# Runs of four: channels and key features interleaved by fours, and sums moved from VectorE to TensorE

## The chip, the core and the metric

One core of a Trainium2 chip runs the whole program. The metric is the device time of one execution in microseconds (us), smaller is better. The engines named are TensorE (PE in the profile; PEld is its weight load), VectorE (DVE), ScalarE (ACT), GpSimd (POOL) and SyncE (SP), which issues the DMAs.

## What is computed

Two branches on the same input `x` (2048 positions, 512 channels, bf16), mixed by a gate per position:

```python
g = sigmoid((x * gate_w).sum(-1))
# A: a convolution along the sequence with a kernel K generated from 128 complex modes per channel
K[d, l] = Re( sum_n C[d,n] * exp(dt[d] * A[d,n] * l) * dt[d] * B[d,n] )
a = causal_conv(x, K) + x * Dskip                 # by FFT of length 4096
# B: linear attention, 32 heads of 16 channels
q, k, v = split(x @ wqkv);  pq, pk = q @ w_phi, k @ w_phi
phi(p) = concat(softmax(p), softmax(-p))          # 16 + 16 features of a head
kv = phi(pk)^T v;  z = phi(pk).sum(over positions)
b = (phi(pq) @ kv) / (phi(pq) @ z + 1e-6) @ wo
out = g * a + (1 - g) * b
```

## The kernel before, in words

The program is written as a plan of 1058 small nodes, each with an engine, its dependences and the buffers that it takes. A string written out by hand, `ORDER` (lines 74 to 95), gives the order in which all nodes are emitted, and so the order of the instructions on each engine; further strings say for some nodes which of two engines (`SIDES`) or which ring of PSUM banks (`RINGS`) they use. Each engine runs its own list strictly in order: an instruction that waits holds up all that stand behind it on that engine.

In order of time, the work is:

- *Preparation* (0 to 30 us): trigonometric tables, transposed input `xT`, folded weights `WW` (`w_phi` multiplied into the key part of `wqkv`).
- *Keys* (`attention_keys`, line 660; 30 to 75 us for the most part, the last pieces at 103 us). Eight passes `s2`, each over two tiles (`u`) of 128 positions. For a tile, `pk` (line 709) is four products of 512 columns into a PSUM bank of the ring `bk` (three banks); `ek` (715) is two exps on ScalarE, of +p and of -p, into the tile's `Ek`. The softmax needs the sum of each head's 16 features. The node `zp` with `ps4` (723) and the node `zk` with `rd` (732) form it, in one of two ways, chosen for each pass by a digit of `ZPS` = "01000111". Digit 1: TensorE adds up four of the sixteen by products with the identity (8 products of 256 columns, line 730), and VectorE reduces the 512 values that are left (739). Digit 0: `zp` issues nothing, and VectorE reduces the 1024 values of each of the two tiles (736). Then `rz` (744): Ln and Exp on ScalarE, the reciprocal of the sums. `vp` (757) is the value product, `vb` its copy, `vr` (766) the values times the reciprocals, and `kn` (774) the 32 products of a tile that add phi(k)^T v into `kvp`, 32 columns of `Ek` as weights each.
- In between, the *input's transform*: `udc` (576) copies half of the channels of the input, with the channels split in two halves `e`, into `UDp`; `psAu` (591) multiplies it with the first FFT stage, 128 columns of `UDp` as weights; `XAu`, `psBu` and `xst` follow, and the result goes to DRAM.
- *Polar tables* (75 to 103 us): `Ctab` and `Dtab`, factors of the convolution kernel's modes, by ScalarE and VectorE. They begin with a ScalarE table load (`tabT`), which in the order stands behind the last `rz` of the keys but one part.
- *Kernel generation and convolution* (103 us to the end). Sixteen units of 32 channels. For a unit, VectorE makes the left factor `A` as two products of 2048 elements, `a1` (1100) and `a2` (1105), and the right factor `R` as two more (1117, 1121) from `E` and `cs`. The product over the modes has four terms. Where the unit's digit in `FOURS` is 1 (units 1, 2, 3, 4, 7, 9, 11 and 12), TensorE adds all four, 128 small products `kps` (line 183, 32 columns of `A` as weights, 64 columns of `R`). Where it is 0 (units 0, 5, 6, 8, 10, 13, 14 and 15), `a3` (1110) first adds the two halves of `A` on VectorE, and TensorE needs 64 products. `KD`, `psA`, `XA`, `psB`, `XK` and `t` (1231) apply the FFT stages and multiply with the input's transform; `psz`, `Zr`, a trip through DRAM (`Zd`, `ZT`) and `psy` turn it back. The attention's query side (`pq`, `Eq`, `zs`, `apm`, `ax`, `ops`) runs between the units, and the output is written at the end.

In memory, `A` is [2 x 2 terms, 4, 8, 32 channels]: the 32 weights of one channel are 32 bf16 values (64 bytes) apart. `UDp` is [2, 64, 32 channels], so its 128 weights are 64 bytes apart too. `Ek` is [2 tiles, 2 signs, 512]: its weights are adjacent.

Of the kernel before, what the change touches and what calls it, by code (L numbers as in the profile page):

```python
# [10 lines left out]
ACT = mybir.ActivationFunctionType  # L11
ALU = mybir.AluOpType
F32 = mybir.dt.float32
BF16 = mybir.dt.bfloat16
# [56 lines left out]
class Plan:  # L71
# [27 lines left out]
             "01111")  # L99
    WARM = ("000000000000000000000000000000000000000000000000000000000000000000000000000000000000000000000000000000000000000000000000"  # L100
            "000000000000000000000")
    FOURS = ("0111100101011000")
    ZPS = ("01000111")

    HOT = ("pk", "vp", "pq", "zp", "ops", "bps4", "psA", "psBu", "psB128", "psB64", "psB32", "psz", "pszn", "psyn32", "psy128", "psy64", "psy32", "kps")

# [68 lines left out]
def kgen_chunk(nc, kps, A, R, four):  # L175

    for e in range(2):
        for g4 in range(4):
            terms = [(k, k) for k in range(2)] if not four else [(0, 0), (2, 0), (1, 1), (3, 1)]
            for i, (ka, kr) in enumerate(terms):  # L180
                for dj in range(4):
                    d = 8 * g4 + 4 * e + dj
                    nc.tensor.matmul(kps[32 * dj:32 * dj + 32, g4, e, :], lhsT=A[:, ka, :, :, d].rearrange("p a b -> p (a b)"),  # L183
                                     rhs=R[:, kr, d, :], start=(i == 0), stop=(i == len(terms) - 1), tile_position=(0, 32 * dj), skip_group_check=True)


# [373 lines left out]
def keys_and_spectrum(P, nc, g, psum):  # L560

    fc, act, at, xT = g.fc, g.act, g.at, g.xT
# [9 lines left out]
    for h in range(2):  # L572
        X = Bag()
        en, uc = [], []
        for k in range(4):
            def cu(h=h, k=k, X=X):
                if k == 0:
                    X.u = g.xau.tile([128, 2, 64, 32], BF16, name="UDp", tag="UDp", bufs=1)
                o = X.u[:, :, 16 * k:16 * k + 16, :].rearrange("p e t c -> p t e c")
                P.copy(o, g.UD[:, 16 * k:16 * k + 16, 64 * h:64 * h + 64].rearrange("p t (e c) -> p t e c", e=2))  # L580
            uc.append(P.add(("DVE", "ACT"), "udc", cu, [sx] + uc[-1:], take=(["UDp"] if k == 0 else []), rw=(f"ud{k}", "")))
        for g4 in range(8):
            box = Bag()

            def pa(h=h, g4=g4, box=box, X=X):
                if g4 == 0:
                    X.t = g.xau.tile([128, 2, 32, 4, 32], BF16, name="XAu", tag="XAu")
                box.ps = psum([128, 4, 256], "psA")
                for i in range(4):
                    c = 4 * g4 + i  # L590
                    nc.tensor.matmul(box.ps[:, i, :], lhsT=X.u[:, :, :, c].rearrange("p e t -> p (e t)"), rhs=fc.W1[:].rearrange("p i r d -> p (i r d)"),  # L591
                                     start=True, stop=True)

            def ea(g4=g4, box=box, X=X):
                i = box.ps[:].rearrange("p c x -> p x c")
                box.ps = None
                return X.t[:, :, :, :, 4 * g4:4 * g4 + 4].rearrange("p i r d c -> p (i r d) c"), i
                if g4 == 7:
                    X.u = None
            a = P.add("PE", "psAu", pa, [a] if g4 else uc, take=["ps"] + (["XAu"] if g4 == 0 else []), drop=(["UDp"] if g4 == 7 else []), rw=("W1", ""))  # L600
            en.append(evict("XAu", ea, [a]))
        eo = []
        for r0 in range(0, 32, 4):
            box = Bag()
# [21 lines left out]
            def wr(h=h, r0=r0, box=box):  # L626
                for n, a in ((128, 0), (64, 128)):
                    nc.sync.dma_start(out=g.XUd[:, h, a:a + n, r0 - 4:r0 + 4, :].rearrange("d x r c -> x d (r c)"), in_=box.s[0:n].rearrange("p d r c -> p d (r c)"))
                box.s = None
            a = P.add("PE", "psBu", pb, en + [a], take=["ps"] + (["xst"] if r0 % 8 == 0 else []), rw=(f"TB0{r0 // 16} TB1{r0 // 16} TBn", ""),  # L630
                      drop=(["XAu"] if r0 == 28 else []))
# [28 lines left out]
def attention_keys(P, nc, g, psum, r):  # L660

    fc, act, at, xT = g.fc, g.act, g.at, g.xT
# [17 lines left out]
    a = P.add("PE", "gps", ga, xt, take=["ps"], rw=("wsm", ""))  # L680
    b = P.add("DVE", "g_b", gb, [a], drop=["psum"])
    b = P.add("ACT", "g_e", lambda: act(out=G.z[:], in_=G.z[:], func=ACT.Exp, scale=-1.0), [b], tab="L")
# [13 lines left out]
    a2 = P.add("PE", "zps", gd, [b] + xt, take=["ps"], rw=("atm", ""))  # L696
# [4 lines left out]
    for s2 in range(8):  # L701
        K = Bag()
        red = []
        for u in range(2):
            box = Bag()
            def pk(st=2 * s2 + u, box=box):
                box.ps = bank("pk")
                for kt in range(4):
                    nc.tensor.matmul(box.ps[:], lhsT=xT[:, st, kt, :], rhs=g.WW[:, kt, :], start=(kt == 0), stop=(kt == 3))  # L709

            def ex(u=u, K=K, box=box):
                if u == 0:
                    K.E = g.kwk.tile([128, 2, 2, 512], BF16, name="Ek")
                for sg in range(2):
                    act(out=K.E[:, u, sg, :], in_=box.ps[:], func=ACT.Exp, scale=(1.0 if sg == 0 else -1.0))
                box.ps = None

            a = P.add("PE", "pk", pk, [a] if u else [sp] + xt + kp, take=["bk"] + ([] if u else ["Ek", "Zk", "vr"]), rw=("TBn", ""))
            x = P.add("ACT", "ek", ex, [a] + ([x] if u else []), drop=["psum"], tab="L")
            red.append(x)  # L720
        box = Bag()

        def ps4(K=K, box=box, on=P.ZPS[s2] == "1"):
            if not on:
                return
            box.ps = bank("zk")
            for u in range(2):
                e = K.E[:, u].rearrange("p g (h a b) -> p (g h) a b", a=4, b=4)
                for k in range(4):
                    nc.tensor.matmul(box.ps[:, 256 * u:256 * u + 256], lhsT=g.ident[:], rhs=e[:, :, k, :], start=(k == 0), stop=(k == 3), skip_group_check=True)  # L730

        def rd(K=K, box=box, on=P.ZPS[s2] == "1"):
            K.Z = g.kwk.tile([128, 2, 2, 32], F32, name="Zk")
            if not on:
                for u in range(2):
                    nc.vector.tensor_reduce(out=K.Z[:, u].rearrange("p g h -> p (g h)"), in_=K.E[:, u].rearrange("p g (h f) -> p (g h) f", f=16),
                                            axis=mybir.AxisListType.X, op=ALU.add)
                return
            nc.vector.tensor_reduce(out=K.Z[:].rearrange("p u g h -> p (u g h)"), in_=box.ps[:].rearrange("p (z b) -> p z b", b=4), axis=mybir.AxisListType.X, op=ALU.add)
            box.ps = None  # L740
        z = P.add("PE", "zp", ps4, red + [a], take=["bk"])
        red = [P.add("DVE", "zk", rd, [z], drop=["psum"])]
# [6 lines left out]
        l = P.add("ACT", "rz", rc, red, drop=["Zk"], tab="L")  # L749
        for u in range(2):  # L750
            box = Bag()
# [18 lines left out]
            def kn(u=u, st=st, K=K):  # L770
                for i in range(8):
                    sg, m = i // 4, i % 4
                    for pr in range(4):
                        nc.tensor.matmul(g.kvp[32 * pr:32 * pr + 32, i, :], lhsT=K.E[:, u, sg, 128 * m + 32 * pr:128 * m + 32 * pr + 32],
                                         rhs=K.v[:, u, sg, :, 8 * m + 2 * pr:8 * m + 2 * pr + 2], start=(st == 0 and i == 0), stop=(st == 15),
                                         tile_position=(0, 32 * pr), skip_group_check=True)
                if u == 1:
                    K.E = K.v = None
            a = P.add("PE", "vp", pv, [a], take=["bk", "vb"], rw=("wv", ""))
            c = evict("vb", cv, [a])  # L780
            c = P.add("DVE", "vr", sc, [c, l], drop=["vb"])
# [278 lines left out]
def plan_conv(P, nc, g, psum, r):  # L1060
# [6 lines left out]
    T, on, yn, late = {}, [], [], []  # L1067
# [20 lines left out]
    def kgen(units, XA, new, split=False):  # L1088
        K = Bag()
        K.done, kps, nu = [], [], len(units)  # L1090
        for cc, U in enumerate(units):
# [3 lines left out]
            c = Bag()  # L1095
            d0 = 32 * U

            def a1(c=c, d0=d0, U=U):
                c.A = g.wk.tile([128, 4, 4, 8, 32], BF16, name="A", tag="A", bufs=g.P.k["A"])
                nc.vector.tensor_tensor(out=c.A[:, 0:2].rearrange("p o a b c -> p (o a) b c"),  # L1100
                                        in0=g.C[U // 8][:, 0:2, :, d0 % 256:d0 % 256 + 32].rearrange("p o a c -> p (o a) c").unsqueeze(2).to_broadcast([128, 8, 8, 32]),
                                        in1=g.D[:, 0, :, d0:d0 + 32].unsqueeze(1).to_broadcast([128, 8, 8, 32]), op=ALU.mult)

            def a2(c=c, d0=d0, U=U):
                nc.vector.tensor_tensor(out=c.A[:, 2:4].rearrange("p o a b c -> p (o a) b c"),  # L1105
                                        in0=g.C[U // 8][:, 1:3, :, d0 % 256:d0 % 256 + 32].rearrange("p o a c -> p (o a) c").unsqueeze(2).to_broadcast([128, 8, 8, 32]),
                                        in1=g.D[:, 1, :, d0:d0 + 32].unsqueeze(1).to_broadcast([128, 8, 8, 32]), op=ALU.mult)

            def a3(c=c):
                nc.vector.tensor_tensor(out=c.A[:, 0:2], in0=c.A[:, 0:2], in1=c.A[:, 2:4], op=ALU.add)  # L1110
            an = [P.add("DVE", "A1", a1, [sh], take=["A"], rw=(Ck + " " + Dk, ""))]
            an.append(P.add("DVE", "A2", a2, an[-1:]))
            an.append(P.add("DVE", "A3", (lambda: None) if four else a3, an[-1:]))
# [512 lines left out]
```

## Time and profile before

| | |
|---|---|
| time of three runs | 264.98, 266.48, 269.46 us (median 266.48) |
| span of the profiled execution, first to last instruction | 265.4 us |
| instructions | 10071 |
| TensorE busy | 208.8 us (79%), 4512 matmuls |
| weight loads busy | 144.6 us (54%) |
| VectorE busy | 233.9 us (88%), 315 instructions |
| ScalarE busy | 221.7 us (84%), 305 instructions |
| mean granted TensorE clock | 0.933 of full speed |

The profile is one execution; its span is 1.1 us below the median of the three timed runs and within their range. "Busy" is the time in which at least one instruction of the engine ran; matmuls are pipelined, so the mean duration of a matmul (some 200 ns and more) is a latency, and the rate is read from the starts. The chain of waits is followed back from the last instruction, at each step to what released it. A group of instructions is written "line engine operation out<-in, sizes, count | busy us, mean ns of one | idle us before them, and what ended most of it".

### The profile page before, as it was taken

The numbers are of one execution on the slowest core, as the hardware profiler recorded it, in microseconds if no ns is written. First come the engines' busy times: TensorE is split into PE (matmuls) and PEld (weight loads), VectorE is DVE, ScalarE is ACT, GpSimd is POOL, SyncE is SP. The second block draws the span as 40 slices with busy tenths as digits, with TensorE's granted clock in tenths as the row PEclk, the third lists the DMA queues.
The fourth block names the chain that finished last, engine by engine and source line by source line (L and its number), as shares of the span: only waits on it lengthen the run. The fifth ranks groups of instructions, "written<-read, shape, count | busy, mean of one in ns | idle before, by whom it ended". The sixth has DMA issues, their size and how long they took to land.

```text
span 265.4 us, 10071 instructions
## 1 busy us (share of the span) xinstructions
PE 208.8 (79%) x4512; PEld 144.6 (54%) x4512; DVE 233.9 (88%) x315; ACT 221.7 (84%) x305; POOL 8.4 (3%) x21
## 2 busy tenths in 40 slices
PE   0768899999964678898857648999997598999760
PEld 0657556655653424447536336775786167965450
DVE  6798898989799989999999999999999798997630
ACT  6989599899899998989999999999999698763300
POOL 4700000000000000000000000000000000000000
PEclk9986799999997579999999999999999799999985
DMA  7799100155510687203243366239753499898776
GB/s 195 130 198 231 23 0 6 63 155 161 145 39 2 195 243 196 84 4 112 73 158 84 100 233 203 76 119 196 160 176 119 167 227 201 207 173 184 161 115 99
DMA packets 67547, 35.93 MB, mean 135 GB/s; under 512 B 46000, under 2 KB 62000, under 8 KB 67504
## 3 DMA queue, kind: packets, MB, share of 16 engines
q1 hardware_dynamic: 65648, 34.76, 53.4%
q8 instruction: 35, 0.57, 1.0%
q10 hardware_dynamic: 1856, 0.52, 1.0%
q14 instruction: 8, 0.07, 0.1%
HBM read 22.17 MB, written 13.11 MB: 133 GB/s over the span
## 4 chain that ended last, share of the span: by engine, by line
PE 39%; DVE 30%; ACT 11%; DMA 9%; issue 7%; SPq 1%; DVEq 0%; ACTq 0%
PE pk L709 6%; PE vp L757 5%; DVE A L1100 4%; DVE R L1121 3%; DVE R L1117 3%; DVE A L1105 3%; DVE Eq L913 3%; PE kps L183 3%; DMA ZT<-Zd 3%; PE psy L824 3%; DMA wqk<-in_B_wqkv_dram 2%; ACT xst L149 2%; DMA ax<-apd 2%; ACT trg L68 2%; PE psA L591 2%
## 5 line engine op out<-in xcount | busy, mean ns | idle before, releaser
L68 ACT ACTIVATE cs<-args 128x1024 bf16<-128x1024 f32 x32 | 30.9, 1052 | 0.9 <-PE args L1023 0.9
L183 PEld LDWEIGHTS <-A 128*32 128x32 bf16 x1536 | 26.4, 161 | 4.8 <-issue 2.0
L183 PE MATMUL kps<-R,A 128*32 128x64 bf16 x1536 | 27.9, 229 | 1.1 <-DVE R L1121 0.7
L1263 PE MATMUL psz<-t,TI 128*128 128x512 bf16 x60 | 16.7, 412 | 5.4 <-DVE t L1231 4.1
L1121 DVE TENSOR_TENSOR R<-E,cs 128x2048 bf16<-128x2048 bf16 x16 | 19.6, 1222 | 0.1
L1105 DVE TENSOR_TENSOR A<-Ctab,Dtab 128x2048 bf16<-128x2048 bf16 x16 | 19.6, 1223 | 0.0
L1100 DVE TENSOR_TENSOR A<-Ctab,Dtab 128x2048 bf16<-128x2048 bf16 x16 | 19.6, 1222 | 0.0
L1117 DVE TENSOR_TENSOR R<-E,cs 128x2048 bf16<-128x2048 bf16 x16 | 19.5, 1220 | 0.0
L149 ACT CAST Zr<-psz 128x1024 bf16<-128x1024 f32 x15 | 15.2, 1022 | 5.1 <-PE psz L1263 3.6
L68 ACT ACTIVATE Ek<-pk 128x512 bf16<-128x512 f32 x32 | 16.7, 601 | 3.2 <-PE pk L709 3.0
L757 PE MATMUL vp<-WW,xT 128*128 128x512 bf16 x64 | 17.8, 419 | 0.0
L1231 DVE TENSOR_TENSOR t<-XUX,XK 128x2048 bf16<-128x2048 bf16 x14 | 16.8, 1222 | 0.4 <-ACT XK L149 0.4
L68 ACT ACTIVATE E<-args 128x1024 bf16<-128x1024 f32 x16 | 16.4, 1036 | 0.6 <-DVE R L1121 0.5
L68 ACT ACTIVATE Eq<-pq 128x512 bf16<-128x512 f32 (+1 forms) x28 | 16.6, 687 | 0.2
L149 ACT CAST XA<-psA 128x1024 bf16<-128x1024 f32 (+1 forms) x15 | 14.6, 1007 | 2.7 <-PE psA L190 2.7
L616 PE MATMUL psB<-XAu,TB 64*128 64x128 bf16 x256 | 11.7, 249 | 6.3 <-ACT XAu L149 3.1
L709 PE MATMUL pk<-WW,xT 128*128 128x512 bf16 x64 | 16.4, 396 | 0.0
L149 ACT CAST XK<-psB 128x1024 bf16<-128x1024 f32 (+1 forms) x14 | 13.7, 990 | 2.5 <-DVE XK L151 1.3
L843 PE MATMUL pq<-xT,Wqp 128*128 128x512 bf16 x64 | 15.5, 380 | 0.2 <-ACT xT L149 0.2
L616 PEld LDWEIGHTS <-TB 64*128 64x128 bf16 x256 | 9.5, 110 | 10.0 <-issue 9.9
L190 PE MATMUL psA<-W,KD 128*64 128x128 bf16 x256 | 9.8, 221 | 5.0 <-ACT cs L68 2.9
L65 ACT ACT_TABLE_LOAD x10 | 12.8, 1283 | 0.1
(211 smaller groups left out, 506.9 us busy)
## 6 DMA issues: line engine op xcount, KB each, us to landing
XUX<-XUd SPq DMA_DIRECT2D x32, 256.0 KB
XUd<-xst SPq DMA_DIRECT2D x8, 512.0 KB
ax<-apd SPq DMA_DIRECT2D x16, 256.0 KB
Zd<-Zr SPq DMA_DIRECT2D x15, 256.0 KB
ZT<-Zd SPq DMA_DIRECT2D x6, 512.0 KB
UD<-in_A_u_dram SPq DMA_DIRECT2D x16, 128.0 KB
XUd<-xst SPq DMA_DIRECT2D x8, 256.0 KB
wqk<-in_B_wqkv_dram SPq DMA_DIRECT2D x1, 1024.0 KB
```

Source lines behind the costliest of these rows:

```text
L68: return self.nc.scalar.activation(**kw)
L149: self.nc.scalar.copy(out=o, in_=i)
L183: nc.tensor.matmul(kps[32 * dj:32 * dj + 32, g4, e, :], lhsT=A[:, ka, :, :, d].rearrange("p a b -> p (a b)"), rhs=R[:, kr, d, :], start=(i ...
L616: nc.tensor.matmul(box.ps[:, c2, sl, :], lhsT=fc.TB[rows, b0:b0 + 2].rearrange("p a b -> p (a b)"), rhs=X.t[rows, k, r0 + sl].rearrange("p ...
L709: nc.tensor.matmul(box.ps[:], lhsT=xT[:, st, kt, :], rhs=g.WW[:, kt, :], start=(kt == 0), stop=(kt == 3))
L757: nc.tensor.matmul(box.ps[:], lhsT=xT[:, st, kt, :], rhs=g.WW[:, 4 + kt, :], start=(kt == 0), stop=(kt == 3))
L1100: nc.vector.tensor_tensor(out=c.A[:, 0:2].rearrange("p o a b c -> p (o a) b c"), in0=g.C[U // 8][:, 0:2, :, d0 % 256:d0 % 256 + 32].rearra ...
L1105: nc.vector.tensor_tensor(out=c.A[:, 2:4].rearrange("p o a b c -> p (o a) b c"), in0=g.C[U // 8][:, 1:3, :, d0 % 256:d0 % 256 + 32].rearra ...
L1117: nc.vector.tensor_tensor(out=c.R[:, :, :, 32:64], in0=t.E[:, 1].unsqueeze(1).to_broadcast([128, 2, 32, 32]), in1=t.cs[:], op=ALU.mult)
L1121: nc.vector.tensor_tensor(out=c.R[:, :, :, 0:32], in0=t.E[:, 0].unsqueeze(1).to_broadcast([128, 2, 32, 32]), in1=t.cs[:, ::-1, :, ::-1], o ...
L1231: nc.vector.tensor_tensor(out=box.t, in0=Ls[r0 // ns].X[:], in1=box.XK[:].unsqueeze(1).to_broadcast([128, 2, 1024]), op=ALU.mult)
L1263: nc.tensor.matmul(box.ps[:, hb, :], lhsT=fc.TI[:, k].rearrange("p t h a -> p (t h a)"), rhs=box.t[:, k, 512 * hb:512 * hb + 512], start=( ...
```

## The change

Three layouts are changed, and with them who adds what. The order string, the engines chosen, the rings and their sizes stay.

- `A` becomes [8 groups of channels, 128 weights, 4 channels]: VectorE's products write runs of four values, and the weights of one channel are 4 values (8 bytes) apart.
- `FOURS` is 1 for all units: `a3` is an empty node everywhere, and every unit's `kps` has 128 products.
- `UDp` becomes [8, 2, 64, 4], in the same way.
- `Ek` becomes [512 features, 2 tiles, 2 signs]: each exp writes single values 8 bytes apart, and `kn`'s weights are 8 bytes apart.
- `ZPS` is gone. In every pass, `zp` adds the 16 features of a head by 16 products with the identity, of 128 columns each, read in runs of four values; `zk` only copies the 128 sums out of PSUM, turning their order.

```diff
-    FOURS = ("0111100101011000")
-    ZPS = ("01000111")
+    FOURS = ("1111111111111111")
...
-  nc.tensor.matmul(kps[...], lhsT=A[:, ka, :, :, d].rearrange("p a b -> p (a b)"),
+  nc.tensor.matmul(kps[...], lhsT=A[:, d // 4, 32 * ka:32 * ka + 32, d % 4],
...
-  X.u = g.xau.tile([128, 2, 64, 32], BF16, name="UDp", tag="UDp", bufs=1)
-  o = X.u[:, :, 16 * k:16 * k + 16, :].rearrange("p e t c -> p t e c")
-  P.copy(o, g.UD[:, 16 * k:16 * k + 16, 64 * h:64 * h + 64].rearrange("p t (e c) -> p t e c", e=2))
+  X.u = g.xau.tile([128, 8, 2, 64, 4], BF16, name="UDp", tag="UDp", bufs=1)
+  o = X.u[:, :, :, 16 * k:16 * k + 16, :].rearrange("p q e t l -> p e q t l")
+  P.copy(o, g.UD[:, 16 * k:16 * k + 16, 64 * h:64 * h + 64].rearrange("p t (e q l) -> p e q t l", e=2, l=4))
...
-  lhsT=X.u[:, :, :, c].rearrange("p e t -> p (e t)")
+  lhsT=X.u[:, c // 4, :, :, c % 4].rearrange("p e t -> p (e t)")
...
-  K.E = g.kwk.tile([128, 2, 2, 512], BF16, name="Ek")
-  act(out=K.E[:, u, sg, :], in_=box.ps[:], func=ACT.Exp, scale=(1.0 if sg == 0 else -1.0))
+  K.E = g.kwk.tile([128, 512, 2, 2], BF16, name="Ek")
+  act(out=K.E[:, :, u, sg], in_=box.ps[:], func=ACT.Exp, scale=(1.0 if sg == 0 else -1.0))
...
-  def ps4(K=K, box=box, on=P.ZPS[s2] == "1"):
-      if not on:
-          return
-      box.ps = bank("zk")
-      for u in range(2):
-          e = K.E[:, u].rearrange("p g (h a b) -> p (g h) a b", a=4, b=4)
-          for k in range(4):
-              nc.tensor.matmul(box.ps[:, 256 * u:256 * u + 256], lhsT=g.ident[:], rhs=e[:, :, k, :], start=(k == 0), stop=(k == 3), skip_group_check=True)
+  def ps4(K=K, box=box):
+      box.ps = bank("zk")
+      e = K.E[:].rearrange("p (h f) u g -> p h f (u g)", f=16)
+      for f in range(16):
+          nc.tensor.matmul(box.ps[:, 0:128], lhsT=g.ident[:], rhs=e[:, :, f, :], start=(f == 0), stop=(f == 15), skip_group_check=True)
...
-      if not on:
-          for u in range(2):
-              nc.vector.tensor_reduce(out=K.Z[:, u]..., in_=K.E[:, u]..., axis=mybir.AxisListType.X, op=ALU.add)
-          return
-      nc.vector.tensor_reduce(out=K.Z[:]..., in_=box.ps[:].rearrange("p (z b) -> p z b", b=4), axis=mybir.AxisListType.X, op=ALU.add)
+      nc.vector.tensor_copy(out=K.Z[:].rearrange("p u g h -> p (u g) h"), in_=box.ps[:, 0:128].rearrange("p (h z) -> p z h", z=4))
...
-  nc.tensor.matmul(g.kvp[...], lhsT=K.E[:, u, sg, 128 * m + 32 * pr:128 * m + 32 * pr + 32],
+  nc.tensor.matmul(g.kvp[...], lhsT=K.E[:, 128 * m + 32 * pr:128 * m + 32 * pr + 32, u, sg],
...
+  def half(k, c=c, d0=d0, U=U):     # a1 is half(0), a2 is half(1)
+      cf = g.C[U // 8][:, k:k + 2, :, d0 % 256:d0 % 256 + 32].rearrange("p o a (q l) -> p (o a) q l", l=4)
+      df = g.D[:, k, :, d0:d0 + 32].rearrange("p b (q l) -> p b q l", l=4)
+      nc.vector.tensor_tensor(out=c.A[:, :, 64 * k:64 * k + 64, :].rearrange("p q (x b) l -> p x b q l", b=8),
+                              in0=cf.unsqueeze(2).to_broadcast([128, 8, 8, 8, 4]), in1=df.unsqueeze(1).to_broadcast([128, 8, 8, 8, 4]), op=ALU.mult)
...
-  c.A = g.wk.tile([128, 4, 4, 8, 32], BF16, name="A", tag="A", bufs=g.P.k["A"])
+  c.A = g.wk.tile([128, 8, 128, 4], BF16, name="A", tag="A", bufs=g.P.k["A"])
```

## The prediction

> **What bounds the kernel now.** I first cut the span into five stretches at places where the chain of waits changes engine, and read the busy time of each engine in each (first column: the stretch in us; then busy us and instruction count by engine).
>
> ```profile
> core 0: us, PE busy (x) PEld busy (x) DVE busy (x) ACT busy (x) POOL busy (x), PEclk, DMA share, GB/s
> 32.04:74.87 42.83, 42.30 (x756) 26.22 (x755) 37.13 (x52) 39.14 (x76) 0.00 (x0) 1.00 0.31 86
> 74.87:102.60 27.73, 18.14 (x264) 10.97 (x264) 26.74 (x48) 26.75 (x30) 0.00 (x0) 0.75 0.44 123
> 102.60:129.80 27.20, 24.06 (x558) 13.82 (x557) 26.96 (x38) 25.95 (x43) 0.00 (x0) 1.00 0.30 98
> 129.80:197.00 67.20, 54.37 (x1329) 40.49 (x1329) 67.10 (x71) 66.37 (x81) 0.00 (x0) 1.00 0.54 144
> 197.00:259.40 62.40, 50.78 (x1446) 37.34 (x1443) 50.38 (x54) 37.80 (x46) 0.00 (x0) 0.95 0.77 172
> ```
>
> The page's total says VectorE is the busiest engine (88%). The stretches say otherwise for this change. From 32 to 75 us (the keys) TensorE has no idle time, at full clock. From 75 to 103 and from 130 to 197 ScalarE is as full as VectorE: 0.98 and 0.83 us idle. Only from 103 to 130 has ScalarE some room, 1.25 us.
>
> The chain of waits through the keys shows why TensorE decides there (start, duration, engine and line).
>
> ```profile
> 55.42 0.97 PE pk L709 x4
> 56.39 0.65 PE kvp L774 x59
> ...
> 71.62 1.85 PE zk L730 x16
> ...
> 73.50 0.70 DVE Zk L739
> ...
> 74.22 0.32 ACT Zk L68
> ...
> 74.88 1.28 ACT L65
> ```
>
> One matmul block follows the other until the last `zk`; then its reduce, Ln and Exp, and the ScalarE table load at 74.88, behind which the tables of the next stretch queue in ScalarE's order. So what TensorE gains in work before 73.5 us moves everything later. The third view is the groups by form: busy us, mean ns of one.
>
> ```profile
> L183 PE MATMUL kps<-R,A 128*32 128x64 bf16 x1536 | 27.9, 229 | 1.1 <-DVE R L1121 0.7 <-ACT XA L149 0.3
> L183 PEld LDWEIGHTS <-A 128*32 128x32 bf16 x1536 | 26.4, 161 | 4.8 <-issue 2.0 <-DVE R L1121 1.2 <-DVE E L1053 0.8
> L774 PEld LDWEIGHTS <-Ek 128*32 128x32 bf16 x512 | 4.9, 100 | 3.4 <-issue 3.2
> L68 ACT ACTIVATE Ek<-pk 128x512 bf16<-128x512 f32 x32 | 16.7, 601 | 3.2 <-PE pk L709 3.0
> L736 DVE TENSOR_REDUCE Zk<-Ek 128x64 f32<-128x1024 bf16 x8 | 9.3, 1210 | 0.0
> L739 DVE TENSOR_REDUCE Zk<-zk 128x128 f32<-128x512 f32 x4 | 2.8, 692 | 1.7 <-PE zk L730 1.6
> L1110 DVE TENSOR_TENSOR A<-A 128x2048 bf16<-128x2048 bf16 x8 | 9.8, 1224 | 0.1
> ```
>
> A load of 32 weight columns takes 161 ns from `A` (columns 64 bytes apart) and 100 ns from `Ek` (adjacent).
>
> **VectorE's part.** Removed: 8 adds L1110, 8 x 1.224 = 9.8 us; 8 reduces L736, 9.7 us; 4 reduces L739, 2.8 us. Added: 8 copies of 128x128 from PSUM at 0.29 us (the 128x128 `den` at L879 takes 0.292), 2.3 us. That is 20 us less. L1100 and L1105 keep their 2048 elements; I keep 1.22 us for them, since `XAu` at L151, which writes runs of four, takes 1218 ns, no more than `xst` at 1222, which writes runs of 32. Both run at half the rate of L1100, so the upper bound is that rate, 2.29 us for 2048; the lower is 1.22.
>
> How much of the 20 us shows? In the keys none: TensorE sets the pace. Of the adds, unit 0's lies at 105 us, those of units 5, 6, 8, 10 between 144 and 194, the last three after 218. From 130 to 197 ScalarE's fixed list takes 66.4 of 67.2 us, so four adds less (4.9 us) buy at most its 0.83 idle; I take 0.4. From 102.6 to 129.8 I take 1.0 of ScalarE's 1.25 idle us: without the add at 104.96 the first R follows 0.6 us earlier, since E ends only at 107.59, and shorter `kps` blocks close the 0.5 us that ScalarE waits near 127. After 197 the chain is DMA (`ax` at 201, `ZT` at 214.5) and then TensorE, and the `kps` of units 14 and 15 start when TensorE is through with `ops` and `psB`, not at the add: nothing. If ScalarE's list were no cover, the five adds would give 5.7 us (third rival).
>
> **TensorE in `kps`.** 128 products take 2.25 us (start 118.70, timeline), 64 take 1.21; without the 0.2 us until the last one ends, 16 ns each. The 64 `kvp` products, with adjacent weights, take 0.72, so 8.2 each. Weights 8 bytes apart are in no row; the bounds are 8.2 and 16. I take 8.2: then four terms cost 128 x 8.2 = 1.05 us where two cost 1.0 and four 2.05. Units 0, 5, 6, 8, 10, 13 to 15 change by nothing, the others give up 1 us each, where ScalarE sets the pace. `UDp`'s loads (146 ns) hide behind 109 ns products already. `kn` reads `Ek` 8 bytes apart too: by the same choice nothing. The row is 161 against 100. The Trainium skill (SBUF — State Buffer, section "Door 1: The DMA port swizzle") states that a stream keeps its full rate if it hits each 16-byte line at least twice. By it the step of 8 bytes is free and the sum below stands; without it, it is that of the second rival.
>
> **TensorE in the keys.** Tiles 0, 2, 3 and 4 of the eight (ZPS bit 0) get a `zk` block that they did not have. A block is 16 products of 128 columns; at L824 and L826 five such start every 0.28 us (163.25, 163.53, 163.81), 56 ns each, so 0.89 us: 4 x 0.89 = +3.56. The other four go from 0.92 to 0.89: -0.12. The blocks also wait for both tiles' exps. Three find them done; tile 4's stands right behind its second `pk` in the order, and its exps run only then:
>
> ```profile
> 55.35 1.04 PE L709 MATMUL pk<-WW,xT 128*128 128x512 bf16 x4
> 56.32 0.72 PE L774 MATMUL kvp<-vr,Ek 128*32 128x34 bf16 x64
> 56.43 1.09 ACT L68 ACTIVATE Ek<-pk 128x512 bf16<-128x512 f32 x2 [0.37 <-PE pk L709]
> ```
>
> TensorE could go on at 56.32 and the exps end at 57.52: +1.20. Behind it in the queue wait `kvp` of tile 3 and the next `pk`, for which the exps of the next tile wait. The four new PSUM tiles take turns in the three `bk` banks; following the ring, each bank is free before its next user arrives. After the last block the copy takes 0.29 where the reduce took 0.69: -0.40.
>
> **ScalarE's exps** write single bf16 values 8 bytes apart instead of a run. No row has that. Nearest are `TI`, ScalarE, 4 bytes apart, with `w` as its contiguous twin, and `SSw`, VectorE, 8 bytes apart:
>
> ```profile
> L68 ACT ACTIVATE TI<-tgsv x2: 261/262/262, 6.0 to 8.2; 128x64 bf16<-128x64 int16 x2
> L68 ACT ACTIVATE w<-tgsv x2: 212/213/214, 5.9 to 7.1; 128x32 bf16<-128x32 int16 x2
> L795 DVE TENSOR_TENSOR SSw<-mask,zcol x1: 310/310/310, 108.1 to 108.1; 128x64 bf16<-128x64 f32 x1
> ```
>
> ScalarE's slope is 0.88 ns an element (601 at 512, 1052 at 1024), so 64 contiguous would take 241, and `TI` pays 21 ns, 0.33 an element: 0.17 us on an exp. VectorE's 128 take 292 and 256 take 422, so 64 would take 227, and `SSw` pays 83 ns, 1.3 an element: 0.66 us on an exp. Bounds 0 and 0.66. I take 0.17, the row of the same engine: 32 x 0.17 = 5.4 us fit into ScalarE's 3.7 idle us and the 4.2 us by which the keys grow, and two pairs (tile 4's, the last) stand on the path: +0.66.
>
> **Sum:** 3.56 - 0.12 + 1.20 - 0.40 + 0.66 = +4.9 until the table load, -1.0, -0.4: +3.5 us. The profiled span is 265.4; the median of the runs, 266.48, stands 1.1 above it. Predicted: 266.5 + 3.5 = 270.0. The copies into `UDp` keep 0.42 us on VectorE; at 1.22 (a plain cast of their size) five would cost 4 us where VectorE has 5.7 idle: nothing.
>
> **Rivals.** (1) *The exps become the bound of the keys.* With 0.66 us more each, ScalarE's work there is 39.1 + 21.3 = 60.4 us in place of a stretch of 42.8: +17.6, less the 1.4 later: 283. ScalarE decides from 0.26 us more per exp on, where 3.7 + 4.9 us of room are used up. For it: the only row with this step. Against: one short instruction, another engine. The Trainium skill (Vector Engine (DVE) Microarchitecture Reference, section "5.2 Measured stream behaviour on trn2 (trn3 not measured)") speaks for it: full rate only for runs of two adjacent 4-byte words, about 2.5 ns for single words a small step apart. `SSw`'s 1.0 + 1.3 ns an element agrees; 2.5 ns on ScalarE (an estimate from that page) would make it 0.83 us more per exp and a time near 289. (2) *Loads 8 bytes apart cost 16 ns.* `kn` grows by 0.5 us per 64 products, six such before 74.9: +3.0; three of the units that go to four terms lie on TensorE's chain after 220: +2.5; 275.5. Against: the slow row has eight times that step. (3) *VectorE alone sets the end after 102*, and ScalarE's full list is only stretched by waits. Then the five adds count, 5.7, and faster `kps` at 184 and 198 another 2.4: 266.5 + 4.9 - 8.1 = 263.3. It decides once ScalarE's starts show gaps of over 4.9 us in all from 102 to 197; they show 2.1. A variant of (1) on VectorE, A's products at 2.29 us, I give only 0.04: 22 of 32 lie before 197, beyond 285.
>
> **Chances.** Forecast 0.47 (its own range 267.5 to 273, the upper quarter of it beyond 2%), rival 1 0.26, rival 2 0.11, rival 3 0.12, A's products 0.04. The range must reach to rival 1 and to rival 3's time: 263.3 to 285 leaves out half of 3, the products and a tenth from the upper end of 1, 0.13 in all; narrower, it would lose a whole case. Two per cent, about what a measurement can tell from no change, is 261.1 to 271.8: faster 0.06 (half of 3), within 0.41 (three quarters of the forecast, the rest of 3), slower 0.53.
>
> **Signs.** Right: `zk` 8 blocks of 16 at 56 ns; a gap before tile 4's block; table load near 79.5; exps near 0.77 us; `kps` at 8 ns a product; ScalarE full from 130 to 200 and VectorE with 4 to 5 us idle there. Wrong: exps over 0.86 us with TensorE idle in the keys; A's loads still near 161 ns; L1100 over 1.3 us; ScalarE's list from the table load to the last `apm` shorter by more than 2 us.

## The result, and the profile after

The changed kernel takes 303.81 us (median of four runs, 302.98 to 304.50) against 266.45 us before: a ratio of 1.143, 95% interval 1.137 to 1.148, slower by 38 us. The forecast was 270.0 us, its range ended at 285. The profiled execution spans 301.7 us. (A median is over all runs of a version, of which some were disturbed and longer, a ratio with its 95% interval is over the undisturbed ones alone, so the two can differ, and a gain or loss in us is worked out from the ratio, times 266.4.)

The same five stages as before the change, cut at the corresponding instructions (busy us and instruction count by engine):

```profile
core 0: us, PE busy (x) PEld busy (x) DVE busy (x) ACT busy (x) POOL busy (x), PEclk, DMA share, GB/s
29.59:95.13 65.54, 49.16 (x841) 32.28 (x849) 27.90 (x49) 59.16 (x76) 0.00 (x0) 0.94 0.21 58
95.13:123.50 28.37, 19.56 (x287) 11.28 (x291) 27.72 (x48) 26.95 (x30) 0.00 (x0) 0.71 0.39 113
123.50:153.45 29.95, 22.74 (x622) 12.17 (x609) 26.23 (x37) 25.93 (x43) 0.00 (x0) 0.98 0.30 93
153.45:226.00 72.55, 54.17 (x1582) 38.35 (x1585) 62.84 (x66) 66.56 (x81) 0.00 (x0) 0.96 0.48 134
226.00:295.70 69.70, 50.16 (x1591) 36.80 (x1595) 46.66 (x50) 37.70 (x46) 0.00 (x0) 0.93 0.72 154
```

Two losses are to be seen. The keys take 65.5 us where they took 42.8, TensorE is busy for only 49.2 of them (42.3 of 42.8 before), and ScalarE, which had 39.1 us of work there, has 59.2. Behind the table load every stage is longer too (28.4, 30.0, 72.6 and 69.7 us against 27.7, 27.2, 67.2 and 62.4), and no engine fills the last three: VectorE has 62.8 us of work in 72.6, ScalarE 66.6.

The chain of waits through the end of the keys, where TensorE blocks used to follow one another:

```profile
81.80 0.98 PE pk L708 x4
82.78 0.02 issue
82.80 9.41 ACT Ek L68 x8
92.21 0.04 issue
92.25 1.87 PE zk L726 x16
```

Eight exps in a row now decide, 9.41 us, 1.18 each. The groups by form (busy us, mean ns of one, idle us before them and what ended it):

```profile
L68 ACT ACTIVATE Ek<-pk 128x512 bf16<-128x512 f32 x32 | 38.1, 1393 | 4.5 <-PE pk L708 4.5
L1092 DVE TENSOR_TENSOR A<-Ctab,Dtab 128x2048 bf16<-128x2048 bf16 x32 | 37.9, 1222 | 4.8 <-PE kps L182 4.2 <-PE args L1014 0.5
L182 PE MATMUL kps<-R,A 128*32 128x64 bf16 x2048 | 22.6, 200 | 11.3 <-issue 10.7 <-ACT XA L148 0.3 <-ACT Zr L148 0.2
L182 PEld LDWEIGHTS <-A 128*32 128x32 bf16 x2048 | 20.2, 116 | 16.3 <-issue 13.4 <-DVE E L1044 1.3 <-DVE R L1114 0.5
L730 DVE COPY Zk<-zk 128x128 f32<-128x128 f32 x8 | 2.3, 292 | 26.8 <-PE zk L726 26.8
```

An exp takes 1393 ns where it took 601 (its whole duration; neighbours overlap, so that they start 1.18 us apart); all 32 keep ScalarE busy for 38.1 us instead of 16.7, 0.67 more each. The weights of `kps` load in 116 ns instead of 161 and TensorE is busy with 2048 products for less time than with 1536 before (22.6 against 27.9 us). But ahead of them stand 10.7 us of idle time that ends with "issue": the engine waited for nothing that a semaphore shows. Such a gap, in the chain of waits:

```profile
145.40 0.57 PE psA L189 x16
145.97 1.35 PE kps L182 x110
147.32 3.19 issue
150.51 0.32 PE kps L182 x11
```

It stands in the middle of one block of 128 products, whose operands had all been there. The DMA view of just this window (147.32 to 150.51 us; packets, MB, share of 16 engines) shows one packet of another kind:

```profile
q1 hardware_dynamic: 289, 0.56, 49.5%
q8 instruction: 1, 0.02, 3.0%
```

That is a load of 16 KB of instructions. The page's queue table counts 39 such packets (35 before), and they follow TensorE: it has some 10200 matmul and load instructions, one packet for each 256. The packet ran from 147.4 to 149.0 us; the products went on 1.5 us later.

The same holds for all such gaps. TensorE has twelve of 0.5 us or more in the trace of the changed kernel, 22.4 us in sum, and in the DMA records each of them ends 1.2 to 1.6 us after the end of an instruction packet; packets start 3.4 us and more apart. In the trace of before there is no such gap.

### The profile page after: what moved, and what is told of

Read it like the earlier page. It is cut to its first block, busy times and chain, and to the rows that moved or that the text cites. A ratio compares the mean times of both kernels' runs of the same rounds, so it can differ in the third digit from the quotient of the medians.

```text
span 301.7 us, 11250 instructions
## 1 busy us (share of the span) xinstructions
PE 212.9 (71%) x5098; PEld 145.7 (48%) x5120; DVE 216.7 (72%) x303; ACT 241.9 (80%) x305; POOL 8.3 (3%) x21
## 4 chain that ended last, share of the span: by engine, by line
ACT 40%; PE 31%; issue 13%; DVE 10%; DMA 4%; POOL 1%; SPq 0%; ACTq 0%; DVEq 0%; POOLq 0%
ACT Ek L68 11%; ACT cs L68 5%; PE kps L182 4%; PE psz L1256 3%; DMA ZT<-Zd 3%; ACT L65 2%; PE psA L189 2%; PE pq L834 2%; ACT xst L148 2%; PE vp L748 2%; PE zk L726 2%; PE psy L815 2%; ACT XA L148 2%; ACT E L68 2%; ACT XAu L148 2%
## 5 line engine op out<-in xcount | busy, mean ns | idle before, releaser
L68 ACT ACTIVATE Ek<-pk 128x512 bf16<-128x512 f32 x32 | 38.1, 1393 | 4.5 <-PE pk L708 4.5
L1092 DVE TENSOR_TENSOR A<-Ctab,Dtab 128x2048 bf16<-128x2048 bf16 x32 | 37.9, 1222 | 4.8 <-PE kps L182 4.2
L182 PE MATMUL kps<-R,A 128*32 128x64 bf16 x2048 | 22.6, 200 | 11.3 <-issue 10.7
L182 PEld LDWEIGHTS <-A 128*32 128x32 bf16 x2048 | 20.2, 116 | 16.3 <-issue 13.4
L730 DVE COPY Zk<-zk 128x128 f32<-128x128 f32 x8 | 2.3, 292 | 26.8 <-PE zk L726 26.8
L148 ACT CAST Zr<-psz 128x1024 bf16<-128x1024 f32 x15 | 15.1, 1024 | 7.8 <-PE psz L1256 7.6
L726 PE MATMUL zk<-Ek,ident 128*128 128x128 bf16 x128 | 10.1, 239 | 13.6 <-ACT Ek L68 13.6
L834 PE MATMUL pq<-xT,Wqp 128*128 128x512 bf16 x64 | 16.5, 396 | 1.4 <-issue 1.3
L1224 DVE TENSOR_TENSOR t<-XUX,XK 128x2048 bf16<-128x2048 bf16 x14 | 16.7, 1219 | 0.7 <-DMA XUX<-XUd 0.7
L726 PEld LDWEIGHTS <-ident 128*128 128x128 bf16 x128 | 9.2, 107 | 16.3 <-issue 15.6
L708 PE MATMUL pk<-WW,xT 128*128 128x512 bf16 x57 | 15.3, 382 | 0.7 <-issue 0.3
L189 PE MATMUL psA<-W,KD 128*64 128x128 bf16 x256 | 11.3, 242 | 4.8 <-ACT cs L68 2.3
```

The source lines that it names most:

```text
L68: return self.nc.scalar.activation(**kw)
L148: self.nc.scalar.copy(out=o, in_=i)
L189: nc.tensor.matmul(ps[64 * ri:64 * ri + 64], lhsT=lhsT, rhs=fc.W1[:, ri].rearrange("p r d -> p (r d)"), start=True, stop=True, tile_positi ...
L726: nc.tensor.matmul(box.ps[:, 0:128], lhsT=g.ident[:], rhs=e[:, :, f, :], start=(f == 0), stop=(f == 15), skip_group_check=True)
L834: nc.tensor.matmul(box.ps[:, m - m0, :] if late else box.ps[:], lhsT=g.Wqp[:, kt, 128 * m:128 * m + 128], rhs=xT[:, 4 * b:4 * b + 4, kt, : ...
L1092: nc.vector.tensor_tensor(out=c.A[:, :, 64 * k:64 * k + 64, :].rearrange("p q (x b) l -> p x b q l", b=8), in0=cf.unsqueeze(2).to_broadcas ...
```

## The experiments

**Which part costs what.** Six versions, with parts of the change put back or done alone.

*Keys as before, the rest as changed* (from the changed kernel):

```diff
-  K.E = g.kwk.tile([128, 512, 2, 2], BF16, name="Ek")
+  K.E = g.kwk.tile([128, 2, 2, 512], BF16, name="Ek")
+  ZPS = ("01000111")
   ... ps4, rd, kn as before
```

> The keys as before the change (Ek contiguous, ZPS 01000111); A, UDp and FOURS as changed. Theory 1 (two separate costs: the exps' spread writes are worth the 20.3 us by which the table load came later, and TensorE's 16 KB instruction loads, one for each 256 instructions, starve blocks of 256 kps instructions that now run in 1.1 us): the table load is back at 75 us, ScalarE's exps at 0.60 us, but the 16 us lost after the table load stay for the most part: 275 to 283 us, with gaps of 1 to 4 us inside kps blocks, 8 us and more in all. Theory 2 (the exps alone; what is lost later follows from the keys being late): 264 to 268 us, as the prediction's -1.4 us has it, and less than 3 us of such gaps.

Measured: 276.15 us, ratio 1.031 (1.022 to 1.040): +8.2 us. The exps are back at 600 ns; the table load is at 73.1 us. At 195 us the kernel is still 1.1 us ahead of before; the loss comes behind that. The pieces of its chain between 196 and 245 us that wait for nothing but "issue":

```profile
197.40 2.31 issue
202.47 0.96 issue
...
214.73 0.85 issue
...
223.22 1.97 issue
240.41 1.60 issue
```

7.7 us in these five, where the same part of before's chain has 0.95 and 0.60 as its longest two and 2.7 us in all. Theory 1's second cost is there without any change in the keys; theory 2 (it follows from late keys) is out. The loss lies at the end of the kernel: from ScalarE's table load near 195 us to the last instruction takes 79.3 us here, 69.6 before.

*Keys changed, the rest as before:*

```diff
-  K.E = g.kwk.tile([128, 2, 2, 512], BF16, name="Ek")
+  K.E = g.kwk.tile([128, 512, 2, 2], BF16, name="Ek")
   ... ps4, rd, kn as changed; A, UDp, FOURS as before
```

> Only the keys are changed (Ek interleaved, 16 products of 128 columns, copies); A, UDp and FOURS as before. Theory 1: table load near 95 us, exps 1.19 us apart, then the stages after it take the 190.5 us that they took before: 284 to 290 us. Theory 2: the whole loss is here, 300 to 305 us.

Measured: 291.67 us, ratio 1.094 (1.087 to 1.101): +25 us, 1.7 above theory 1's range, far under theory 2's. The table load comes at 94.8 us, 19.9 late. Some 4 to 5 us are lost behind it, with TensorE gaps of 9.7 us in sum, one of 3.2 us inside `kps` at 161.7 us.

*Only the layouts of `A` and `UDp`:*

```diff
-  FOURS = ("1111111111111111")
+  FOURS = ("0111100101011000")
   ... on the version with the keys as before
```

> The keys and FOURS as before; only the layouts of A and UDp (runs of four) are changed, with the third product a3 on the new layout in eight units. TensorE has as many instructions as before the change. Theory 1: kps at 8 ns a product, yet units with four terms still burst through 256 instructions: 265 to 270 us, gaps in kps of 2 to 6 us. Theory 2: 264 to 267 us, no gaps to speak of.

Measured: 266.74 us, ratio 1.002 (0.998 to 1.007). The time lies in both theories' ranges; TensorE's gaps add up to 2.1 us, one of 1.2 inside `kps`, nearer to theory 2. Loads that are a quarter shorter and a TensorE that is 7 us less busy (201.9 against 208.8) buy nothing that can be measured.

*`FOURS` alone, old layout of `A`:*

```diff
-  FOURS = ("0111100101011000")
+  FOURS = ("1111111111111111")
   ... on the kernel before
```

> Before's kernel with FOURS 1 for all units: 512 more products and 512 more loads on TensorE, eight adds less on VectorE, the old layout of A (16 ns a product). Theory 1: as many instruction loads as the keys-back version has, about 39, but a block of 256 instructions takes 2.25 us instead of 1.1, so the gaps inside kps shrink by about 1 us each, and TensorE's own work grows by 8 us: 270 to 282 us. Theory 2 (instruction loads cost nothing; ScalarE's list sets the pace): 264 to 270 us.

Measured: 275.65 us, ratio 1.031 (1.024 to 1.039): +8.3 us, within theory 1's range and as much as with the new layout. Here too the loss is at the end (77.2 us from the table load near 195 us, against 69.6). The granted clock does not explain it: it is 0.938 in this profile, 0.933 before, and 0.912 in the version with the layouts alone, which loses nothing. The groups of the version with the keys as before, and of this one:

```profile
L183 PE MATMUL kps<-R,A 128*32 128x64 bf16 x2048 | 23.7, 204 | 7.7 <-issue 6.8 <-ACT Zr L149 0.4 <-ACT XA L149 0.3
L183 PEld LDWEIGHTS <-A 128*32 128x32 bf16 x2048 | 21.0, 118 | 12.7 <-issue 10.9 <-DVE R L1123 0.7 <-DVE E L1053 0.4
```

```profile
L183 PE MATMUL kps<-R,A 128*32 128x64 bf16 x2048 | 37.0, 230 | 3.8 <-issue 3.0 <-ACT XA L149 0.3 <-ACT Zr L149 0.2
L183 PEld LDWEIGHTS <-A 128*32 128x32 bf16 x2048 | 35.0, 161 | 8.2 <-issue 6.1 <-DVE R L1121 0.7 <-DVE A L1105 0.6
```

13 us more work in the second, 4 us less waiting for "issue", the same time in the end. What both have in common is 39 instruction loads. In the first version the products' own time is not what the 8 us are: `kps` keeps TensorE busy for 4 us less than before, and the gaps add up to 10.9 us. In the second it may be a part: 9 us more work in `kps` than before, and 5.7 us of gaps. That the two totals agree does not show that they have the same make-up.

*TensorE's sums in all eight passes, `Ek` contiguous:*

```diff
-  ZPS = ("01000111")
+  ZPS = ("11111111")
   ... on the kernel before
```

> Before's kernel with ZPS 1 in all eight passes: Ek stays contiguous, TensorE gets the four zk blocks (8 products of 256 columns) that it did not have, VectorE loses eight reduces of 1.21 us and gets four of 0.69. This is the prediction's key stage without the exps' price: 4 x 0.92 + 1.2 (the stall at tile 4's block) = +4.9 us at the table load. Theory 1 (the prediction's terms for TensorE were right, the exps' price was what failed): table load at 79 to 81 us, 269 to 273 us in all. Theory 2 (TensorE has more room in the keys than its busy time shows): table load at 75 to 77 us, 265 to 268 us.

Measured: 270.80 us, ratio 1.021 (1.014 to 1.027): +5.5 us, within theory 1's range. Its table load is at 77.0 us, the upper end of theory 2's range and not in theory 1's. What that means is less sure than it looks: before and the ten versions with the keys of before add up the keys in the same way, and their profiles have the table load anywhere from 71.8 to 75.5 us, 73.4 in the mean. So this one is 1.5 to 5.2 us late, 3.6 from the mean, and before's own 74.9 is on the late side. Behind it TensorE has 4.1 us of gaps, for which the expectation had nothing.

*All of the change but the spread write* (this `ZPS` on the version with the keys as before, `FOURS` 1 for all):

```diff
-  ZPS = ("01000111")
+  ZPS = ("11111111")
   ... FOURS, A, UDp as changed
```

> The whole change except the spread write: A, UDp and FOURS as changed, Ek contiguous as before, and the sums of all eight passes on TensorE in before's form (8 products of 256 columns, VectorE reduces the rest). Theory 1 (the parts add up: +4.3 us for TensorE's sums in the keys, +9.7 us for the products of all units, the rest of the 37.4 us is the exps' spread write): 277 to 284 us, table load at 76 to 79 us. Theory 2 (with the keys later, most of the loss behind them stays whatever the exps cost): 290 us and more.

Measured: 283.70 us, ratio 1.064 (1.056 to 1.072): +17.0 us, within theory 1's range, though 3.3 more than the two parts by themselves (5.5 + 8.2), which the three intervals together (some 3.6) do not tell from none. What is left to the full change is (1.143 - 1.064) x 266.4 = 21 us, 0.66 us for each of the 32 exps. It carries more than the spread write: the full change also adds with 16 products of 128 columns instead of 8 of 256, 64 products and 64 loads more in all, and `kn` reads its weights 8 bytes apart. Keys only against sums only, a pair with the same differences, gives (1.094 - 1.021) x 266.4 = 19 us.

**The two disputed costs by themselves.** A small program of two parts, run once:

```diff
+  for o in (Erun, Estep4B, Estep8B, Eruns2, Eruns4, Ef32step8B):   # 4 times each
+      act(out=o, in_=pk, func=ACT.Exp);  ... and vector.tensor_copy(out=o, in_=pk)
+  blocks(kquiet, 12)          # 12 x 128 products, 32 weight columns, 64 moving columns
+  dma_start(...) x 6          # 12 MB of writes
+  blocks(kbusy, 12)
```

> Not the kernel: a small program of two parts, no part of the reference is computed. (a) The disputed write by itself: 512 exps from PSUM on ScalarE, and the same as copies on VectorE, into six layouts, four times each: a run; single bf16 4 bytes apart; single bf16 8 bytes apart; runs of two every 8 bytes; runs of four every 32 bytes; single f32 8 bytes apart. (b) 12 blocks of 128 products with 32 adjacent weight columns and 64 moving columns (256 TensorE instructions a block), once with no DMA traffic and once beside a stream of DMA writes. Theory 1: exps 0.52 us apart into a run, 1.19 us into single values 8 bytes apart; at 4 bytes apart about 0.7; runs of two and of four between 0.52 and 0.7. TensorE uses up the instructions that lie ready at 8 ns a product and is then held to one 16 KB load of 256 instructions every 3 to 4 us, with gaps of 2 to 3 us, with and without the DMA stream. Theory 2 (loads of instructions cost nothing by themselves, only DMA traffic delays them): the first 12 blocks go at 8 ns a product throughout (12.6 us), gaps only beside the stream.

The timeline of ScalarE (start, us, of 4 or 8 exps; "Eruns" holds the runs of two and those of four):

```profile
9.58 2.48 ACT L85 ACTIVATE Erun<-pk 128x512 bf16<-128x512 f32 x4 [7.57 <-PE pk L72]
11.96 3.07 ACT L85 ACTIVATE Estep4B<-pk 128x512 bf16<-128x512 f32 x4
14.90 5.30 ACT L85 ACTIVATE Estep8B<-pk 128x512 bf16<-128x512 f32 x4
19.94 4.94 ACT L85 ACTIVATE Eruns<-pk 128x512 bf16<-128x512 f32 x8
24.78 2.63 ACT L85 ACTIVATE Ef32step8B<-pk 128x512 f32<-128x512 f32 x4
```

0.62 us each into a run, 0.77 for single bf16 values 4 bytes apart, 1.33 at 8 bytes, and 0.62 again for runs of two every 8 bytes and runs of four every 32 (one mean for both). Single f32 values 8 bytes apart cost 0.66, next to nothing. On VectorE much the same: 691 ns, 725, 1291, 692 and 689. So it is single 2-byte values at this step that are slow, on both engines.

The timeline of TensorE, without DMA traffic and beside it:

```profile
24.86 1.90 PE L94 MATMUL kquiet<-x 128*32 128x64 bf16 x128 [1.56 <-issue]
28.59 1.90 PE L94 MATMUL kquiet<-x 128*32 128x64 bf16 x128 [1.83 <-issue]
32.04 1.90 PE L94 MATMUL kquiet<-x 128*32 128x64 bf16 x128 [1.55 <-issue]
...
61.98 1.90 PE L94 MATMUL kbusy<-x 128*32 128x64 bf16 x128 [5.94 <-issue]
69.82 1.90 PE L94 MATMUL kbusy<-x 128*32 128x64 bf16 x128 [5.94 <-issue]
```

A block of 256 instructions, 1.90 us at this program's clock (0.58), comes every 3.5 to 4.0 us while no DMA but the loads themselves runs, and every 7.3 to 7.8 us beside writes of 418 GB/s. The DMA view of 23.3 to 44.6 us has one line, a load every 3.55 us:

```profile
q8 instruction: 6, 0.10, 1.8%
```

Every gap in this program, too, ends 1.2 to 1.6 us after the end of such a load. Theory 1 said "with and without the stream", which fits; its gaps of 2 to 3 us were 1.6 to 2.1 us here, its 8 ns a product some 15 ns, and that the stream doubles the time, it did not say. Theory 2's 12.6 us for twelve free-running blocks are out.

**Instructions or their work.** The rest asks whether the 8.2 us of `FOURS` are a matter of the number of TensorE instructions, and of their place.

*`FOURS` 0 again for the last three units:*

```diff
-  FOURS = ("1111111111111111")
+  FOURS = ("1111111111111000")
   ... on the version with the keys as before
```

> The keys as before; A and UDp as changed; FOURS 1 for units 0 to 12 and 0 for the last three (13, 14, 15), where a3 is back on VectorE and kps has 64 products. The keys-back version reaches the table load at 195 us 1.1 us earlier than before and loses all its 9.7 us behind it. Theory 1 (TensorE's chain at the end pays for each extra instruction there, by the instruction loads): with the last three units at 64 products the loss goes: 263 to 267 us. Theory 2 (the loss comes from the five units in the middle, whose extra instructions shift all later loads): 270 to 276 us.

Measured: 270.49 us, but ratio 1.006 (0.999 to 1.012), +1.5 us: between the two ranges, nearer to theory 1's. With 384 instructions fewer than the version with the keys as before, and three adds more on VectorE, 6.7 of its 8.2 us are gone; in its profile the stretch from the table load near 195 us (here at 198.3) takes 70.7 us, close to before's 69.6.

*Idle instructions in those units, and in three in the middle* (on the kernel before; the real products overwrite what they leave):

```diff
+  for j in range(8):        # per group: 64 products a unit, one moving column
+      matmul(kps[32*(j%4):..., g4, e, 0:1], lhsT=A[:, 0, 0, j, :], rhs=R[:, 0, 0, 0:1], ...)
   ... for U in (13, 14, 15); in the second version for U in (0, 5, 6)
```

> Before's kernel; kps of the last three units (13, 14, 15) gets 64 idle products more each (one moving column, weights adjacent, overwritten by the real ones): 384 TensorE instructions and at most 1.6 us of TensorE's time (192 x 8.2 ns), nothing else. Theory 1 (instructions are what costs there; with 64 real products more, these units cost 6.7 us): 271 to 276 us. Theory 2 (work or VectorE's list costs): 266 to 268 us.

> The same 384 idle instructions in units 0, 5 and 6, which lie between 104 and 160 us, where ScalarE and VectorE are full and TensorE has room. Theory 1 (TensorE's gaps hide behind the full engines there, but the edges of the loads move): 265 to 270 us, less than in the last three units. Theory 2 (the place does not matter): the same as in the last three units.

Measured: 269.97 us, ratio 1.016 (1.006 to 1.027), and 271.47 us, ratio 1.013 (1.005 to 1.022). 384 instructions that do next to nothing cost 4.3 and 3.5 us, more than their 1.6 us of time. In the last units that lies between the two theories' ranges, under the 5 us that theory 1 asked for as a minimum; so the instructions alone account for part of the 6.7 us that 192 real products cost there, as far as these wide intervals tell. And the place makes no difference that these intervals show: theory 1's "less in the middle" is not borne out.

*Idle transposes in TensorE's first wait*, 64 and 96 of them on the kernel before, 64 on two others:

```diff
+  for _ in range(64):       # 128 instructions while TensorE waits for the first DMA
+      nc.tensor.transpose(out=box.ps[:, 0, 0:128], in_=g.ident[:], identity=g.ident[:])
```

> Before's kernel with 64 idle transposes (128 TensorE instructions, overwritten results) put into the first 7.9 us, in which TensorE waits for the first DMA; all else is as before. They move the edges of the 256-instruction loads by half a load against the work. Theory 1 (where a load's edge falls in a dense block decides the size of the gaps): the time moves by 1 to 4 us, up or down, with other gaps than before. Theory 2: idle work costs nothing, within 0.5% of before.

> Before's kernel with 96 idle transposes (192 TensorE instructions) in the first 7.9 us, where the shift by 128 gave 269.3. Theory 1 (the edges of the 256-instruction loads decide): another time again, 264 to 271 us, with the gaps inside or ahead of the kps blocks elsewhere than with 128. Theory 2 (the idle work itself costs): 1.5 times the loss of 128, 270.5 us, with the same gaps.

> The keys as before, all else as changed (276.2 us), with 64 idle transposes (128 TensorE instructions) in the first 7.9 us. Theory 1 (number of instructions in the tail costs, the edges add or take a few us): 271 to 281 us. Theory 2 (the 9.7 us are only an unlucky place of the edges): 264 to 269 us.

> Only the keys changed (291.7 us), with 64 idle transposes (128 TensorE instructions) in the first 7.9 us. The table load of that version came 20.3 us late, the end 25.2 us. Theory 1 (the 5 us between are gaps where a load's edge meets a dense block): with the edges moved by half a load the time moves by 1 to 5 us, and the 3.2 us gap in kps near 162 us goes elsewhere or away; the table load stays near 95 us. Theory 2 (the 5 us belong to the late keys): 290 to 293 us.

Measured: 64 on the kernel before 269.31 us, ratio 1.014 (1.008 to 1.021), with gaps of 2.1 us inside `psA` and 1.6 inside `kps`, at 186 and 202 us, that before does not have. 96: 271.06 us, ratio 1.014 (1.004 to 1.023); that half as many again cost more is not shown, nor excluded. The version with the keys as before: 274.05 us, ratio 1.031 (1.025 to 1.037), unchanged: at this one other place of the loads' edges its 8 us are still there, and the 128 idle instructions cost it nothing that shows. Keys only: 292.58 us (288.08 to 293.65), which these four runs do not tell from its 291.67 (289.84 to 293.61). As theory 1 had it, the 3.2 us gap in `kps` is gone from the trace, and the stretch between the two table loads at 97.8 and 219.7 us is 3.3 us shorter than the 125.1 without the shift, but the first of them comes 3.1 us later. Whether the shift helps this version is left open.

*A candidate*, the layouts of `A` and `UDp` with one unit less of four terms:

```diff
-  FOURS = ("0111100101011000")
+  FOURS = ("0111100101010000")
```

> A candidate for a faster kernel: layouts of A and UDp as changed, keys as before, FOURS as before but 0 for unit 12 too, whose kps stands on TensorE's chain at 198 us: 128 TensorE instructions less there, one more add of 1.22 us on VectorE near 190 us. Theory 1 (each instruction less behind 195 us counts): 262 to 266 us. Theory 2 (VectorE's add is on the chain there, or the loads' edges fall worse): 266 to 270 us.

Measured: 268.01 us, ratio 1.006 (1.001 to 1.011), 1.6 us slower. That is outside theory 1's range of 262 to 266 us. 128 instructions less did not help here; none of the versions tried beats the kernel before.

## Why the prediction was wrong

**The exps (rival 1, given 0.26).** The term "32 x 0.17" failed. I had two rows, +0.33 ns an element from `TI` and +1.3 from `SSw`, and took "the row of the same engine". The small program shows that the engine did not matter and the step did: `TI` writes 4 bytes apart, which costs 0.15 us on 512 values; `SSw` writes 8 bytes apart, which costs 0.6 to 0.7 on either engine. The upper bound, 0.66, was the value (0.67 by the busy times; that the difference between the versions gives 0.66 as well is partly chance, as it carries other things and an interval of some 0.08). And the step from the price to the path failed with it: the forecast let all but two pairs of exps hide in ScalarE's idle time, and instead ScalarE's list became what decides in the keys, 59.2 us of work, with TensorE waiting 13.6 us in all for exps ahead of its `zk` blocks. Rival 1 had this mechanism and put the keys at +17.6; the table load came 20.3 us later, since ScalarE still waited for `pk` (4.5 us in the groups above) at stalls like the one ahead of tile 4's block, which was 3.29 us instead of the 1.2 of the forecast.

On what I cited for it: 1.29 to 1.33 us for 512 values are 2.5 to 2.6 ns a value, the figure that the Trainium skill (Vector Engine (DVE) Microarchitecture Reference, "5.2 Measured stream behaviour on trn2 (trn3 not measured)") gives for single words a small step apart, and ScalarE shows it as well; but single f32 values 8 bytes apart went at full rate on VectorE (689 ns against 691) and nearly so on ScalarE. The rule of the Trainium skill (SBUF — State Buffer, "Door 1: The DMA port swizzle"), two hits in each 16-byte line, held nearly for the weights (116 ns a load, 100 adjacent, 161 at 64 bytes) and for those f32 writes, and failed for 2-byte writes, which also hit each line twice.

**TensorE in the keys.** 16 products of 56 ns, the 0.29 us copies and the need for both tiles' exps were right. TensorE's sums alone gave +5.5 us where 4 x 0.92 + 1.2 = 4.9 was asked, but the agreement is in part luck: the 4.9 were all to come before the table load, which came 3.6 us later than the mean of the profiles with unchanged keys and 2.1 later than before's. The rest lies behind it, where the forecast had no loss. (The sum puts the forecast's table load at 74.9 + 4.9 = 79.8 us; its list of signs says 79.5.) `kn` at no cost was nearly right: its loads take 116 ns instead of 100, and its products 6.5 us instead of 6.3.

**`kps`.** "8.2 ns", with four terms at 1.05 us where two cost 1.0, was right as a rate: an undisturbed block takes 1.26 us, without the 0.2 us until its last product ends 8.4 ns a product. From it I concluded that units 0, 5, 6, 8, 10 and 13 to 15 "change by nothing", and that step failed: it priced 512 products by their time on the array and their 1024 instructions at nothing. They cost 8.2 us, the same with products of 16 ns and of 8. In the sum the stage from 102.6 to 197 was to gain 1.4 us and what follows 197 (the tail) nothing; the version with the keys as before lost 0.7 from its table load to 195 us and the rest in the tail. There, 7.7 us of its gaps stand on the chain of waits. That ScalarE's list paces the middle, and that five adds less on VectorE therefore buy next to nothing, held in that version (121.6 us between the two table loads, 120.9 before, with 117.5 and 117.8 us of work on ScalarE). In the full change it did not hold: the same stretch took 129.6 us with 118.2 us of work on ScalarE, and TensorE's waits for "issue" in it add up to 11.7 us.

**`A`'s products** at 1222 ns in runs of four: right. **`UDp`**: its loads fell from 146 to 123 ns behind products that hide them.

**The account.** Sums on TensorE +5.5, four terms everywhere +8.2, 3.3 more when both are together (not clear of the intervals), the spread write and what goes with it 21: 38 us. The forecast had 4.2 of the first, -1.4 for the second, 0.7 of the last. That the gaps are waits for instruction loads is shown by the packets, in this kernel and in the small program. The gaps of 0.5 us and more add up to nothing before, 2.1 us with the layouts alone, 4.1 with the sums alone, 5.7 and 10.9 in the two versions with four terms everywhere, 9.7 with the keys only and 22.4 in the full change. How much of each loss they are stays open, since some of them hide behind other engines. Open, too, is when TensorE asks for the next 256 instructions and what delays them inside this kernel. On the kernel before, idle instructions cost 9 to 30 ns each (384, 192 and 128 of them); on the version with the keys as before 128 cost nothing that shows. The small program's rate is 14 ns an instruction without other DMA traffic and 30 beside it.

## What to carry over

Price a write by its element size and step before its engine: a layout that makes the reader's access dense may leave the writer with single 2-byte values, and a run of two was enough to make them free. Where many tiny matmuls are added, count instructions as well as nanoseconds: halving the time of each of 2048 products bought nothing, and adding 512 cost 8 us. Read what an engine's work is worth in the stage where it lies: with five adds less on VectorE, the version with the keys as before was no faster through the middle, where ScalarE's list is as full.

## What was not expected of the hardware

TensorE's instructions arrive in loads of 256, in a dense run of small products one every 3.5 to 4.0 us without other DMA traffic and 7.3 to 7.8 us beside 418 GB/s of DMA writes, and a block that uses them up in 1.3 to 1.9 us stands still until 1.2 to 1.7 us after the end of the next packet; in the changed kernel such gaps were 0.9 to 4.4 us long. Writing 512 single bf16 values costs 0.62 us in a run, 0.77 at 4 bytes, 1.33 at 8 bytes, on ScalarE; on VectorE 0.69, 0.73 and 1.29; single f32 values at 8 bytes cost 0.66 and 0.69.
